# Twelve late result buffers, a written-out end of attention and two routings in turn, in a fused attention and mixture-of-experts kernel

## The chip, the cores and the metric

The kernel runs on one core of a Trainium2 chip. The metric is the device time of one execution in microseconds (us). A core has several engines, each of which works off its own program in order: TensorE (PE) multiplies matrices and transposes, VectorE (DVE) and ScalarE (ACT) do elementwise work and reductions, GpSimd (POOL) does some elementwise work and issues DMAs, SyncE (SP) issues DMAs. Engines wait for one another, and for DMAs, at semaphores. In the profile a name such as SPq or ACTq is the queue on which an engine issues its transfers.

## What is computed

The reference has two parts. Attention works in chunks of 32 queries, each with 16 keys of left context, 8 of right context and 8 memory keys (B=4 batches, H=8 heads, S=768 positions, D=64). Its output, seen as x with N=3072 rows of 512 columns, goes through a router that picks two of E=8 experts for each token, and each expert is a two-layer network with 1024 hidden units:

```python
scores = scale * np.matmul(q_c, k_full.transpose(0, 1, 3, 2))
a = softmax(scores)                      # in the reference: max, exp, divide
out[:, :, c_start:c_end] = np.matmul(a, v_full)
...
x = attn_out.transpose(0, 2, 1, 3).reshape(B * S, H * D)
noisy_logits = x @ w_gate + np.log1p(np.exp(x @ w_noise)) * noise
top2 = np.argpartition(-noisy_logits, 2, axis=1)[:, :2]
top2_w = softmax(take_along_axis(noisy_logits, top2, axis=1))
for e in range(E):
    for k in range(2):
        mask = top2[:, k] == e
        h = np.maximum(x[mask] @ w1[e], 0.0)
        out[mask] += top2_w[mask, k, None] * (h @ w2[e])
```

## The kernel before

The whole body runs under a manual schedule: the order in which the code issues instructions is the order on each engine, and the framework only adds the waits between engines and hands out buffers from pools. When a pool's tile has several buffers (bufs=6), the writer of the seventh tile waits for the last reader of the first.

*Attention* runs over 16 pairs of heads (four per batch), as a pipeline in the loop at L754. A turn i of the loop issues the transposes of the probabilities of pair i-1 (PT_pe, with the copy PT_copy on ACT), the maximum and the subtraction of pair i (max_dve), transposes of q and k of pair i+2 (turn_pe), the product with v of pair i-1 (PV_pe), the exponential of pair i (exp_act), the router's logits of pair i-3 (logits_pe), the normalising multiply of pair i-1 (mult_dve), the transposes of the finished rows of pair i-2 (xT_pe) and the scores of pair i+1 (scores_pe). It also loads v on POOL's queue, and the first experts' weights at turns 10, 12 and 14. The loop has a 17th turn (i=16) in which only the parts for earlier pairs run.

*Routing* follows whenever four pairs of a batch have their logits (route, L353). It is cut into small steps: s1 exponential and logarithm on ACT; s1b, s2 noisy logits and their comparison on DVE; s2b which experts come first and second; s2c, s2d the gates' exponentials; s3 on PE the rank of every token in its expert's queue, which needs the counts of the batches before (`seen`); s4 the gates into the row and the store of the batch's rows to a table in DRAM (x_rows, L421; on SP's queue for batches 0 to 2, on ACT's for batch 3); s4b, s5, s5b, s5c ranks into slots (s5c on POOL); s6 on PE the table of which token sits in which slot; s7 its copy; s8 the update of `seen`, with `gap`, which closes slots that later batches may not use. For batches 0 to 2 these steps wait in a list (`pending`), from which steps() (L567) takes one or two groups per turn.

*Experts.* Each expert has 832 slots: six tiles of 128 and a seventh of 64. decode (L536) makes indices from the table. gather (L594) fetches a tile's rows from x_rows by an indirect DMA that POOL issues; 14 buffers hold what was fetched. turn (L611) transposes a tile on PE and copies it out on ACT or DVE, up (L634) is the first layer with its relu (from three PSUM banks, alternately on ACT and DVE), down (L652) the second layer: per tile eight matmuls into one of two banks, an eviction with the gate into a result tile `ys` (L660, six buffers; ACT for odd tiles at L672, DVE for even ones at L674), and a scatter-add of that tile into `out`, an indirect DMA on POOL (L675). The generator every (L690) orders all this. Experts 0 and 1 start before routing is complete: tiles 0 and 1 from batches 0 and 1 (idx_s), tiles 2 and 3 after batch 2 (idx_a), tiles 4 to 6 after batch 3 (idx_f). Experts 2 to 7 follow with seven tiles each; gathers run ahead by two to three sets, first-layer weights are loaded in down, second-layer weights between the gathers. units(k) takes k steps of this generator, so that expert work can be put between steps of routing by hand.

*Around the end of attention* (L798 to L833) the order in code is: after the last turn the PSUM banks of attention are given to the experts; decode for batch 2, the middle gathers (L807), the zero fills of `out` (L809: three DMAs of 2 MB on SP's queue from a zero tile zt), w2 of expert 1 (L811), the last logits, the turns of expert 1's first tiles on DVE, then batch 3's routing in five groups with expert units in between (L818), the half tile's fix, decode for all, and the gathers of sets 2 and 3. Then a new pool ("full", L838) takes the memory that attention's pool leaves.

*Overflow.* Between the second layers of sets 6 and 7, L843 to L859 find tokens that did not fit: `gov` is read back from the gate columns of x_rows (L849, a DMA on SP's queue), multiplied by `miss` (L851) and stored back (L872). A loop at the end (L884) would work on such tokens; with these inputs it ends at once.

Of the kernel before, what the change touches and what calls it, by code (L numbers as in the profile page):

```python
# [24 lines left out]
def kernel(  # L25
# [44 lines left out]
    SKIP = 32  # L70
    NEG = -1e30
# [16 lines left out]
    def body():  # L88
# [243 lines left out]
        def xT_pe(n):  # L332
# [4 lines left out]
            xt = ap_.tile([128, BT, 128], BF16, name="xt")  # L337
# [15 lines left out]
        def route(b):  # L353
# [61 lines left out]
            def s4():  # L415
# [5 lines left out]
                (nc.sync if b < B - 1 else nc.scalar).dma_start(out=xd_part[b][b * S:(b + 1) * S].rearrange("(t p) r -> p t r", p=128), in_=xrows[b])  # L421
# [49 lines left out]
            def s8():  # L471
# [8 lines left out]
                if b >= B - 3:  # L480
# [8 lines left out]
            if b == B - 1:  # L489
                return (s1,), (s1b, s2), (s2b, s3, s2c, s4b, s5, s5c), (s2d,), (s4, s5b), (s6, s7)  # L490
            if b == B - 3:
                return (s1,), (s1b, s2), (s2b, s2c, s2d), (s3, s4, s4b, spare_a), (s5, s5c, spare_b), (s5b, spare_c), (s6, s7, s8, spare_d, begin_first)
# [141 lines left out]
        def up(s, c0=0, c1=None):  # L634
# [5 lines left out]
            k = -(-(c1 - c0) // 512)  # L640
            for f in range(FB):
# [10 lines left out]
        def down(s, between=()):  # L652
            e, tiles = sets[s]
            ht = hts[s]
            for n, j in enumerate(tiles):
# [4 lines left out]
                ys = mp.tile([128, Dm], F32, name="ys", bufs=6)  # L660
# [93 lines left out]
        for i in range(NPAIR + 1):  # L754
# [4 lines left out]
            if i < NPAIR:  # L759
                max_dve(i)  # L760
# [4 lines left out]
            if i < NPAIR:  # L765
                steps(1)
            if i >= 1:
                PV_pe(i - 1)
            if i < NPAIR:
                exp_act(i)  # L770
            if i >= 3:
                logits_pe(i - 3)
                if (i - 3) % HP == HP - 1:
                    begin, *rest = route((i - 3) // HP)
                    begin[0]()
                    assert not pending
                    pending.extend(rest)
# [4 lines left out]
            if i >= 2:  # L782
                xT_pe(i - 2)
# [12 lines left out]
            steps(1 if i < NPAIR - 2 else 2)  # L796
            if i >= NPAIR - 1:
                units(FB // 2)  # L798
        assert not pending
        pctx.close()  # L800
# [4 lines left out]
        turns["ring"] = bankT[:2]  # L805
        decode(tabs[(B - 2) % 2][:, :EARLY * NT], idx_a, None)
        for s in range(EARLY):  # L807
            gather(s, range(FIRST, SEALED), idx_a)
        for x in range(3):  # L809
            zero_fill(8 * x, 8)  # L810
        load_w2(1)  # L811
        logits_pe(NPAIR - 2)
        xT_pe(NPAIR - 1)
        cnt["by"] = "dve"
        for j in range(FIRST):
            turn(1, j)
        logits_pe(NPAIR - 1)
        begin, *rest = route(B - 1)  # L818
        begin[0]()
        units(3)  # L820
        cnt["by"] = "act"
        for g, more in zip(rest, (3, 4, 1, 4, 1)):
            for fn in g:
                fn()
# [136 lines left out]
```

## Time and profile before

| what | value |
|---|---|
| three runs, us | 346.88, 347.7, 351.45 (median 347.7) |
| profiled execution, us | 351.4, of which 349.3 are the span of the core's instructions |
| mean granted TensorE clock | 0.928 |
| busy, share of the span | PE 79%, DVE 46%, ACT 43%, POOL 66% |
| DMA | 60.30 MB, mean 173 GB/s |

All positions in time below are us from the start of the profiled execution's span. A row of the timeline gives start, duration, engine, line and operation, then output<-inputs by the program's names with the shape, and in brackets the time that the engine was idle before it with what ended that wait. A row of the waits gives engine, tile and line, what released it, and then the total, the count and the longest. A row of the DMA issues gives the KB of one transfer and the median time from issue to landing. PEclk on the page is the TensorE clock that the throttle granted, in tenths of full speed, for 40 equal slices of the span.

### The profile page before, as it was taken

The numbers are of one execution on the slowest core, as the hardware profiler recorded it, in microseconds if no ns is written. First come the engines' busy times: TensorE is split into PE (matmuls) and PEld (weight loads), VectorE is DVE, ScalarE is ACT, GpSimd is POOL, SyncE is SP. The second block draws the span as 40 slices with busy tenths as digits, with TensorE's granted clock in tenths as the row PEclk, the third lists the DMA queues.
The fourth block names the chain that finished last, engine by engine and source line by source line (L and its number), as shares of the span: only waits on it lengthen the run. The fifth ranks groups of instructions, "written<-read, shape, count | busy, mean of one in ns | idle before, by whom it ended". The sixth has DMA issues, their size and how long they took to land. (4 is left out here: it accounts for less than half of the span.)

```text
span 349.3 us, 7639 instructions
## 1 busy us (share of the span) xinstructions
PE 277.5 (79%) x3071; PEld 175.5 (50%) x3085; DVE 161.4 (46%) x363; ACT 149.1 (43%) x295; POOL 228.9 (66%) x219
## 2 busy tenths in 40 slices
PE   0787687686667758795999999399999999999940
PEld 0765566575455545353555555255555555545420
DVE  7467569789784664221434343033343433324310
ACT  1689978868444543212343433223332432223110
POOL 8997777548323512787878686887887825656380
PEclk9999969969676999998999999889999999999995
DMA  9999999999989997499989999999999997959293
GB/s 113 161 149 186 164 166 186 195 127 213 185 154 376 380 226 143 96 140 226 209 161 190 214 195 211 204 175 193 202 200 192 179 145 111 124 65 139 27 138 45
DMA packets 99110, 60.30 MB, mean 173 GB/s; under 512 B 63488, under 2 KB 83968, under 8 KB 99072
## 3 DMA queue, kind: packets, MB, share of 16 engines
q0 software_dynamic: 82208, 49.84, 105.2%
q1 hardware_dynamic: 15792, 9.05, 9.0%
q10 hardware_dynamic: 1072, 0.88, 0.8%
q8 instruction: 26, 0.43, 0.5%
q14 instruction: 12, 0.10, 0.1%
HBM read 65.07 MB, written 23.27 MB: 253 GB/s over the span
## 5 line engine op out<-in xcount | busy, mean ns | idle before, releaser
L647 PEld LDWEIGHTS <-w1t 128*128 128x128 bf16 x576 | 57.5, 101 | 52.9 <-issue 11.8
L675 POOL DMA_INDIRECT out_dram<-ys,idx_f x40 | 62.8, 1570 | 31.8 <-DVE ys L674 20.7
L603 POOL DMA_INDIRECT xl<-x_rows,idx_f x48 | 49.8, 1037 | 28.7 <-DVE hts L632 10.8
L663 PE MATMUL bankE<-w2t,htf 128*128 128x512 bf16 x278 | 65.7, 379 | 0.5
L647 PE MATMUL bankE<-xTf,w1t 128*128 128x416 bf16 x256 | 52.0, 346 | 5.4 <-DVE xTf L624 5.4
L674 DVE TENSOR_SCALAR ys<-bankE,gt 128x512 f32<-128x512 f32 (+1 forms) x32 | 21.9, 684 | 69.3 <-PE bankE L663 49.8
L672 ACT ACTIVATE ys<-bankE,gt 128x512 f32<-128x512 f32 x24 | 16.5, 687 | 71.4 <-PE bankE L663 52.5
L133 POOL DMA_DIRECT2D vp<-in_v_dram x34 | 33.3, 987 | 15.3 <-PE bankO L316 4.9
L663 PEld LDWEIGHTS <-htf 128*128 128x128 bf16 x288 | 27.3, 98 | 28.8 <-issue 0.3
L630 ACT ACTIVATE htf<-bankE 128x416 bf16<-128x416 f32 x32 | 16.5, 517 | 34.7 <-PE bankE L647 34.7
L632 DVE TENSOR_SCALAR htf<-bankE 128x416 bf16<-128x416 f32 x32 | 18.9, 591 | 26.9 <-PE bankE L647 26.9
L647 PE MATMUL bankT<-xTf,w1t 128*128 128x416 bf16 x128 | 28.4, 345 | 0.3 <-DVE htf L632 0.3
L263 ACT COPY kT<-bankT 64x768 bf16<-64x768 bf16 x32 | 25.3, 791 | 6.2 <-PE bankT L253 5.8
L620 PE MATMUL bankT<-identb,xl 128*128 128x128 bf16 (+1 forms) x224 | 20.3, 219 | 5.5 <-DMA xl<-x_rows,idx_f 2.3
L620 PEld LDWEIGHTS <-xl 128*128 128x128 bf16 (+1 forms) x224 | 15.3, 99 | 16.1 <-issue 4.4
L663 PE MATMUL bankE<-w2t,hts 128*128 128x512 bf16 x92 | 21.5, 379 | 0.2
L647 PE MATMUL bankT<-xTs,w1t 128*128 128x256 bf16 (+1 forms) x88 | 15.2, 314 | 5.8 <-ACT hts L630 4.2
L287 DVE TENSOR_REDUCE mx<-bankS 128x12 f32<-128x768 f32 x16 | 15.2, 953 | 9.3 <-PE bankS L282 9.3
L647 PE MATMUL bankE<-xTs,w1t 128*128 128x256 bf16 (+1 forms) x104 | 16.0, 297 | 2.6 <-DVE xTs L624 1.3
L313 PE MATMUL bankO<-memv,PT 128*128 128x132 bf16 x96 | 9.9, 251 | 9.8 <-ACT PT L306 9.6
L289 DVE TENSOR_TENSOR sd<-bankS,mx 128x768 f32<-128x768 f32 x16 | 15.3, 958 | 1.8 <-DVE mx L287 0.5
L455 POOL TENSOR_TENSOR col<-mm_all,tl 128x672 f16<-128x672 f16 x4 | 6.7, 1670 | 14.4 <-DVE tl L442 14.4
(182 smaller groups left out, 456.0 us busy)
## 6 DMA issues: line engine op xcount, KB each, us to landing
w1t<-in_moe_w_dram POOLq DMA_DIRECT2D x8, 1024.0 KB, 12.1
w2t<-in_moe_w_dram POOLq DMA_DIRECT2D x8, 1024.0 KB, 11.3
out_dram<-zt SPq DMA_DIRECT2D x3, 2048.0 KB, 10.3
vp<-in_v_dram POOLq DMA_DIRECT2D x30, 168.0 KB, 8.6
qg<-in_q_dram POOLq DMA_DIRECT2D x16, 192.0 KB, 7.7
kg<-in_k_dram POOLq DMA_DIRECT2D x16, 192.0 KB, 8.0
x_rows<-xrow SPq DMA_DIRECT2D x3, 792.0 KB, 8.3
x_rows<-xrow ACTq DMA_DIRECT2D x1, 792.0 KB
```

What stands on the lines that cost most here:

```text
L133: nc.gpsimd.dma_start(out=vp[p0 + j:p0 + j + nj, c:c + m, hh, :], in_=bass.AP(v.tensor, v.offset + (hd * S + c * chunk + j - left_ctx) * D ...
L263: nc.scalar.copy(kbufs[n % 2][hs, hh].rearrange("d (p j) -> d p j", j=SJ), p_t[hs])
L289: nc.vector.tensor_tensor(out=sd, in0=st[n]["ps"], in1=mx.rearrange("p x (u o) -> p x u o", o=1).to_broadcast([128, 2, BT, CTX]), op=Alu.s ...
L603: nc.gpsimd.indirect_dma_start(out=xl, out_offset=None, in_=xd, in_offset=bass.IndirectOffsetOnAxis(ap=idx[:, c:c + 1], axis=0), bounds_ch ...
L620: nc.tensor.transpose(out=p_t[:, kp, :w], in_=xl[:w, kp * 64:(kp + 1) * 64].bitcast(BF16), identity=identb[:w, :w])
L630: nc.scalar.activation(out=dst, in_=src, func=Act.Relu)
L632: nc.vector.tensor_scalar(out=dst, in0=src, scalar1=0.0, scalar2=None, op0=Alu.max)
L647: nc.tensor.matmul(out=h[:, :hi - lo], lhsT=W1[e][:, kp, f * 128:(f + 1) * 128], rhs=xTs[s][:, kp, lo:hi], start=(kp == 0), stop=(kp == KP ...
L663: nc.tensor.matmul(out=y, lhsT=ht[:, f, o:o + w], rhs=W2[e][:, f, :], start=(f == 0), stop=(f == FB - 1))
L672: nc.scalar.activation(out=ys[:, :wide], in_=y[:, :wide], func=Act.Copy, scale=gate)
L674: nc.vector.tensor_scalar(out=ys[:, :wide], in0=y[:, :wide], scalar1=gate, scalar2=None, op0=Alu.mult)
L675: ins = nc.gpsimd.indirect_dma_start(out=rows, out_offset=bass.IndirectOffsetOnAxis(ap=idx, axis=0), in_=ys[:, :wide], in_offset=None, bou ...
```

## The change

Twelve result buffers instead of six, in the pool "full". Batch 3's rows are stored on SP's queue instead of ACT's. The update of `seen` (s8) is separated from `gap` (s8b), and for batch 1 it comes one group earlier. In up(), two blocks of at most 256 columns share a PSUM bank and one relu instruction, so a unit of the narrow sets now covers two blocks. The attention loop ends after turn 15; what turn 16 did is written out behind it, ahead of expert work, and the steps of batch 2's and batch 3's routing are called by name, in turn with the remaining parts of attention and with units. The zero fills are issued in the code at turn 14 (NPAIR - 2), and their only wait is for zt. The turns of expert 1's first tiles are no longer forced to DVE ahead of batch 3's routing; those of expert 0 stand between the last parts of attention. `gov` is set to zero on DVE before it is read back. The loop for tokens that did not fit takes its accumulator from another pool.

```diff
@@ -68,6 +68,7 @@
...
     SKIP = 32
+    NYS = 12
     NEG = -1e30
@@ -334,7 +335,7 @@
...
                 nc.tensor.transpose(out=p_x[:, t, :], in_=xrows[b][:, t, hp * 64:(hp + 1) * 64].bitcast(BF16), identity=identb)
-            xt = ap_.tile([128, BT, 128], BF16, name="xt")
+            xt = ap_.tile([128, BT, 128], BF16, name="xt", bufs=3)
             nc.scalar.copy(xt, p_x)
@@ -418,7 +419,7 @@
...
                 nc.vector.tensor_tensor(out=xrows[b][:, :, XC:].bitcast(F32), in0=ge, in1=bc(gs, E), op=Alu.mult)
-                (nc.sync if b < B - 1 else nc.scalar).dma_start(out=xd_part[b][b * S:(b + 1) * S].rearrange("(t p) r -> p t r", p=128), in_=xrows[b])
+                nc.sync.dma_start(out=xd_part[b][b * S:(b + 1) * S].rearrange("(t p) r -> p t r", p=128), in_=xrows[b])
@@ -477,7 +478,9 @@
...
                     nc.vector.tensor_copy(seen, sm)
-                if b >= B - 3:
+
+            def s8b():
+                if B - 3 <= b < B - 1:
@@ -486,10 +489,10 @@
...
-            if b == B - 1:
-                return (s1,), (s1b, s2), (s2b, s3, s2c, s4b, s5, s5c), (s2d,), (s4, s5b), (s6, s7)
+            if b >= B - 2:
+                return dict(s1=s1, s1b=s1b, s2=s2, s2b=s2b, s2c=s2c, s2d=s2d, s3=s3, s4=s4, s4b=s4b, s5=s5, s5b=s5b, s5c=s5c, s6=s6, s7=s7, s8=s8, s8b=s8b)
             if b == B - 3:
-                return (s1,), (s1b, s2), (s2b, s2c, s2d), (s3, s4, s4b, spare_a), (s5, s5c, spare_b), (s5b, spare_c), (s6, s7, s8, spare_d, begin_first)
+                return (s1,), (s1b, s2), (s2b, s2c, s2d), (s3, s4, s4b, spare_a), (s5, s5c, spare_b), (s5b, spare_c, s8), (s6, s7, s8b, spare_d, begin_first)
             return (s1,), (s1b, s2), (s2b, s2c, s2d), (s3, s4, s4b), (s5, s5c), (s5b,), (s6, s7, s8)
@@ -638,6 +641,18 @@
...
             k = -(-(c1 - c0) // 512)
+            w = c1 - c0
+            if 2 * w <= 512:
+                for f in range(0, FB, 2):
+                    h = hring[cnt["h"] % 3] if hring else tr()
+                    cnt["h"] += 1
+                    for x in range(2):
+                        for kp in range(KP):
+                            nc.tensor.matmul(out=h[:, x * w:(x + 1) * w], lhsT=W1[e][:, kp, (f + x) * 128:(f + x + 1) * 128], rhs=xTs[s][:, kp, c0:c1],
+                                             start=(kp == 0), stop=(kp == KP - 1))
+                    relu(hts[s][:, f:f + 2, c0:c1], h[:, :2 * w].rearrange("p (x w) -> p x w", w=w))
+                    yield "up", s, f
+                return
             for f in range(FB):
@@ -657,7 +672,7 @@
...
                 gate = gts[s][:, j:j + 1]
-                ys = mp.tile([128, Dm], F32, name="ys", bufs=6)
+                ys = pools["full"].tile([128, Dm], F32, name="ys", bufs=NYS)
                 if w == CAP:
@@ -751,35 +766,38 @@
...
                 scores_pe(0)
-        for i in range(NPAIR + 1):
+        late = {}
+        for i in range(NPAIR):
             if i + NQ < NPAIR:
...
                 PT_pe(i - 1)
-            if i < NPAIR:
-                max_dve(i)
+            max_dve(i)
             if i >= 1:
...
                 turn_pe(i + 2, 0)
-            if i < NPAIR:
-                steps(1)
+            steps(1)
             if i >= 1:
                 PV_pe(i - 1)
-            if i < NPAIR:
-                exp_act(i)
-            if i >= 3:
+            exp_act(i)
+            if 3 <= i < NPAIR - 1:
                 logits_pe(i - 3)
                 if (i - 3) % HP == HP - 1:
-                    begin, *rest = route((i - 3) // HP)
-                    begin[0]()
-                    assert not pending
-                    pending.extend(rest)
+                    b = (i - 3) // HP
+                    if b == B - 2:
+                        late[b] = route(b)
+                        late[b]["s1"]()
+                    else:
+                        begin, *rest = route(b)
+                        begin[0]()
+                        assert not pending
+                        pending.extend(rest)
             if i + 2 < NPAIR:
...
                 mult_dve(i - 1)
-            if i >= 2:
+            if 2 <= i < NPAIR - 1:
                 xT_pe(i - 2)
@@ -793,36 +811,56 @@
...
                 load_w2(0)
-            steps(1 if i < NPAIR - 2 else 2)
-            if i >= NPAIR - 1:
-                units(FB // 2)
+                for x in range(3):
+                    zero_fill(8 * x, 8)
+            steps(1)
         assert not pending
+
+        def do(r, *names):
+            for nm in names:
+                r[nm]()
+
+        n = NPAIR - 1
+        r2 = late[B - 2]
+        PT_pe(n)
+        PT_copy(n)
+        xT_pe(n - 2)
+        do(r2, "s1b", "s2")
+        PV_pe(n)
+        mult_dve(n)
+        xT_pe(n - 1)
+        logits_pe(n - 3)
+        logits_pe(n - 2)
         pctx.close()
...
         turns["ring"] = bankT[:2]
+        do(r2, "s2b", "s2c")
+        turn(0, 0)
+        xT_pe(n)
+        logits_pe(n - 1)
+        do(r2, "s3", "s4b", "s8")
+        turn(0, 1)
+        do(r2, "s2d")
+        logits_pe(n)
+        r3 = route(B - 1)
+        do(r3, "s1")
+        do(r2, "s5", "s5c", "s8b", "s5b", "s4")
+        units(4)
+        do(r2, "s6", "s7")
         decode(tabs[(B - 2) % 2][:, :EARLY * NT], idx_a, None)
...
             gather(s, range(FIRST, SEALED), idx_a)
-        for x in range(3):
-            zero_fill(8 * x, 8)
         load_w2(1)
-        logits_pe(NPAIR - 2)
-        xT_pe(NPAIR - 1)
-        cnt["by"] = "dve"
-        for j in range(FIRST):
-            turn(1, j)
-        logits_pe(NPAIR - 1)
-        begin, *rest = route(B - 1)
-        begin[0]()
+        do(r3, "s1b", "s2", "s2b", "s2c")
+        units(4)
+        do(r3, "s3", "s4b", "s2d", "s5", "s5c", "s4")
         units(3)
-        cnt["by"] = "act"
-        for g, more in zip(rest, (3, 4, 1, 4, 1)):
-            for fn in g:
-                fn()
-            units(more)
+        do(r3, "s5b")
+        units(1)
+        do(r3, "s6", "s7")
         tab = tabs[(B - 1) % 2]
@@ -846,6 +884,7 @@
...
         gov = lp.tile([128, NP, E], F32, name="gov")
+        nc.vector.memset(gov, 0.0)
         nc.sync.dma_start(out=gov, in_=xd[:, XC:].rearrange("(t p) e -> p t e", p=128).bitcast(F32))
@@ -903,7 +942,7 @@
...
             bounds_check=N - 1, oob_is_err=True)
-        o = mp.tile([128, Dm], F32, name="ys", bufs=6)
+        o = lp.tile([128, Dm], F32, name="o")
         nc.gpsimd.indirect_dma_start(
...
             bounds_check=N - 1, oob_is_err=True)
```

## The prediction, made before the changed kernel was run

> **What bounds the kernel now.** I read the page's slices first, then the waits of TensorE (PE), then the timeline around each long wait, then GpSimd's (POOL's) timeline and the DMA issues. From 137.6 to the end PE is busy in nearly every slice, so what it waits for there is time. The waits of PE after 100 us: line, what ended the wait, total, times, longest.
>
> ```profile
> PE bankE L647 <- DVE xTf L624: 5.4, 1, 5.4
> PE bankT L647 <- ACT hts L630: 4.2, 1, 4.2
> PE bankT L620 <- DMA xl<-x_rows,idx_f: 2.3, 3, 1.3
> ```
>
> The two long ones are named after a relu and a copy, but the timeline shows what these were late for (start, duration, engine; in brackets the idle time before it and its releaser).
>
> ```profile
> 160.60 0.69 ACT L672 ACTIVATE ys<-bankE,gt 128x512 f32<-128x512 f32 x1 [7.52 <-DMA out_dram<-ys,idx_a]
> ...
> 161.67 0.79 PE L647 MATMUL bankT<-xTs,w1t 128*128 128x320 bf16 x4 [4.23 <-ACT hts L630]
> ```
>
> ```profile
> 225.67 0.48 DVE L674 TENSOR_SCALAR ys<-bankE,gt 128x256 f32<-128x256 f32 x1 [7.74 <-DMA out_dram<-ys,idx_f]
> ...
> 226.41 2.96 PE L647 MATMUL bankE<-xTf,w1t 128*128 128x416 bf16 x8 [5.40 <-DVE xTf L624]
> ...
> 229.16 1.49 PE L647 MATMUL bankT<-xTf,w1t 128*128 128x416 bf16 x4
> ```
>
> An eviction waits for a result buffer (ys, six of them) whose scatter has not landed; copies and relus queue behind it, and PE behind these. The scatters are late because POOL issues without a gap, one per 1.87 us, from the first final gather at 137.55 to 281:
>
> ```profile
> 224.31 1.57 POOL L675 DMA_INDIRECT out_dram<-ys,idx_f  x1 [0.30 <-issue]
> ...
> 226.19 1.56 POOL L675 DMA_INDIRECT out_dram<-ys,idx_f  x1 [0.30 <-issue]
> ```
>
> What starts that sequence is the end of routing. Batch 2's rows are stored at 103.81, zero fills follow on the same queue, the middle gathers go at 116.50, batch 3's rows at 129.32, and the final gathers when these have landed:
>
> ```profile
> 103.81 0.36 SPq L421 DMA_DIRECT2D x_rows<-xrow  x1
> ...
> 104.26 5.45 SPq L576 DMA_DIRECT2D out_dram<-zt  x3
> ...
> 116.50 1.12 POOL L603 DMA_INDIRECT xl<-x_rows,idx_a  x1 [7.23 <-DVE idx_a L546]
> ...
> 129.32 0.41 ACTq L421 DMA_DIRECT2D x_rows<-xrow  x1
> ...
> 137.55 1.13 POOL L603 DMA_INDIRECT xl<-x_rows,idx_f  x1 [10.78 <-DVE hts L632]
> ```
>
> A late stretch matters for the added memset. VectorE (DVE) does the overflow bookkeeping between two expert layers, and PE loses 0.30 us there; the read of gov had been issued at 136.96, long before:
>
> ```profile
> 278.00 0.36 DVE L851 TENSOR_TENSOR gov<-gov,miss 128x192 f32<-128x192 f32 x1
> ...
> 278.86 0.58 DVE L632 TENSOR_SCALAR htf<-bankT 128x416 bf16<-128x416 f32 x1
> ...
> 279.50 0.86 PE L647 MATMUL bankT<-xTf,w1t 128*128 128x416 bf16 x4 [0.30 <-DVE htf L632]
> ```
>
> DMA prices (KB each, median us to landing):
>
> ```profile
> w2t<-in_moe_w_dram POOLq DMA_DIRECT2D x8, 1024.0 KB, 11.3
> out_dram<-zt SPq DMA_DIRECT2D x3, 2048.0 KB, 10.3
> x_rows<-xrow SPq DMA_DIRECT2D x3, 792.0 KB, 8.3
> nz_all<-in_moe_noise_dram SPq DMA_DIRECT2D x1, 96.0 KB, 5.8
> x_rows<-gov SPq DMA_DIRECT2D x1, 96.0 KB, 6.1
> ```
>
> **The change part by part.** The sum is made against the profiled execution: 351.4 us, of which 349.3 are the span. The three runs shown have a median of 347.7, 3.7 less; I take that off at the end.
>
> *Twelve ys buffers.* Both waits go: the writer then needs the scatter twelve tiles back, which by POOL's order had been issued 27 us or more before in both places. Gone are 4.23 and 5.40. After each, PE also ran at half clock for a while: four groups of 320 columns took 161.67 to 165.45, 3.78, where later ones take 0.54 each (2.15), so 1.6 more; three groups of 416 took 226.41 to 230.49, 4.08 for 2.11, so 2.0 more. Together 13.2. What is late next are the gathers, for POOL's work is the same and only starts with the stage. The seventh gather of expert 2 went out at 163.88 and landed 6.6 later, 170.5; PE used it at about 176.9. Moved by the stage's 4.1 (below) it lands at 166.4, and PE, earlier by 4.1 and 5.8, asks at 167.0; the ones before it land at 169.4 to 170.2 and are asked for two tiles earlier. I charge 1.0. The next sets land 1.5 us or more ahead. The new pool lies in memory that attention used; its last user, batch 3's row store, lands at about 133, before the first ys: nothing. Net -12.2.
>
> *End of attention.* Until 98.2 (multiply of pair 13) little changes; the earlier `seen` may save up to 1.2, not counted. Then DVE skipped from pair 14 to 2.9 us of batch 2's routing before pair 15's reduction; now pair 15 goes first. Reduction and subtraction (0.95, 0.96) end at 100.1, exp (0.84) at 101.0, transposes and copy (0.5, 0.8) at 102.3, PV (1.0) at 103.3, multiply (0.23, 0.96) at 104.5; pair 14's multiply and four routing steps fill DVE's gaps. Batch 2 still needs, on DVE in order: 1.4 (over to gd), 0.25 (rk), 0.4 (seen), 1.4 (r_all to tl), 0.6 (gap), 1.75 (Rn), 0.8 (ge to xrow): 6.6. Its row store leaves at 111.1, 7.3 later than before. Then transfers follow one another: landing 6.5 (this store took 5.7; the slowest of its kind 9.3), the first middle gather at 117.9, the fourth 4.05 later, landing 3.2 (a gather in an empty queue took 2.8 to 3.2, the middle ones beside the zero fills up to 7.7), and only now batch 3's store, which must wait for those gathers because it writes the table they read: 125.2. Its own DVE work (1.2, 2.9, 2.0 and 0.8 after 111.1) ends at 118, so the store no longer waits for it. Landing 8.0 as before (129.32 to 137.3; expert 1's w2t load is beside it again), issue 0.3: final gathers at 133.5 instead of 137.55, -4.1. With the shortest landings (5.7, 2.8, 5.7) it is -7.6, with the longest (9.3, 6.3, 9.3) +3.1. PE's first use of them moves alike.
>
> *Zero fills.* Their only wait is for zt (22.3), so SP issues them right behind batch 1's store, at 79.5, not at pair 14. SP has nothing else until 111. They now lie beside the v load of the last pair (83.83, landed after 8.7, used at 102.3), w1t of expert 1 (86.51, 11.5), the first gathers (92.1 to 96.3, used at 104) and w2t (97.3). Beside them a w2t load took 13.0 instead of 11.3, gathers up to 4 more: covered, 0; at worst 2, when the first gathers land after 104. At 111 the queue is free again if they sustain half the 400 GB/s they had from 108 to 120. The Trainium skill (DMA: Bandwidth & Descriptors, section Queues, rings and completion order) says each engine serves its queues in turn, a packet each. By it a load beside the fills would take up to twice as long, w1t 23 instead of 11.5, and land at 109.5, still before its use at 112: the sum would be the same, only the margin smaller.
>
> *Memset of gov.* The read now waits for it, and the memset stands in DVE's order behind the sixth full down-projection, so the read starts there and the multiply waits for it on DVE. Behind it wait four small operations and every second relu of the next layer; PE stops after the three banks are full, where it already lost 0.30. The read has 24 rows of 32 bytes per partition; the nearest rows of that shape are 5.8 (nz_all) and 6.1 (the store of gov), and I take 6.1. The memset (about 0.2) and the add of 0.36 beside it cancel: +6.0, and PE's half clock after such a wait another 2.0, as above: +8.0. Bounds: 2.8 (quickest gather), which costs 2.7 and no slow clock, and 12.5 (slowest v load), 14.4. The skill's price for one DMA (same page, section Anatomy of one DMA) is 2.0 us and bytes over 436 GB/s, 2.2 for these 96 KB; the sum would then be 5.9 us less.
>
> *The rest.* Relus of two blocks in one instruction: 16 of 512 columns for 32 of 256 (0.38 each), on ScalarE while PE needs 0.87 for the pair: covered, 0. The store moved from ACT's queue to SP's frees 0.41 of ACT: 0. POOL's order is the same throughout.
>
> Sum: -13.2 + 1.0 - 4.1 + 8.0 = -8.3: 343.1 against the profiled execution, 339.4 against the median.
>
> **The rivals.** (A) The gov read is quick or hidden: 2.2 to 3 us instead of 6.1, about 5.5 less, 334. For it: no other traffic on SP's queue. Against: both rows of that shape. (B) The end of attention gains nothing: three transfers in a chain where DVE work stood before, each with a long landing, +3.1 instead of -4.1: 346.6. For it: a store of 9.3 and gathers of 7.7 exist; against: these had heavy neighbours. (C) POOL is the bound, and the buffers only change what PE waits for. From 137.55 to 281 POOL has no gap, so each gather comes when POOL gets to it. If the gathers of experts 2 and 3 landed late enough to give back all 13.2, what is left is -4.1 + 8.0: 351.6, slower. It decides from 8.3 us of such waits on; against it stand the landings above, which leave at most 1. (D) The memory of the new pool makes the first evictions wait for attention's last readers: then ys at 135 waits some us; priced with B.
>
> **How the numbers follow.** Forecast 0.50; A 0.18; B (with D) 0.20; C 0.12. The forecast alone spans 336 to 343. The range reaches from A's lower part to B's upper one, 332 to 347. Two per cent, about what a measurement here tells from no change, is 340.7 and 354.7. Faster: two thirds of the forecast and A, 0.52; slower: the worse half of C, 0.06; the same: 0.42.
>
> **What would show it.** No eviction waits for out_dram near 157 or 221, and PE runs through; final gathers near 133.5, batch 2's store near 111, batch 3's 14 us behind it; zero fills at 79.5; one DVE wait of 6 us in gov's multiply, with PE idle about as long behind it and half clock after. Wrong would be: gathers named as PE's releaser for over 2 us in the full layers, a gov wait under 3, or a start of the final gathers after 138.

## The result, and the profile after the change

The changed kernel takes 360.56 us (median of four runs, 357.64 to 362.15); the kernel before, with one more run beside it, 348.62 (346.88 to 351.45). The ratio is 1.0325, 95% interval 1.0217 to 1.0433: slower by 3%, where 339.4 us were forecast. The profiled execution took 359.07 us, its span 357.4; before these were 351.4 and 349.3, so 8.1 us are to be found in the traces.

The waits of TensorE from 80 us on (columns as before: line, what ended the wait, total, times, longest):

```profile
PE bankE L662 <- DVE htf L635: 12.4, 1, 12.4
PE bankO L317 <- DMA vp<-in_v_dram: 7.5, 2, 4.4
PE bankT L623 <- DMA xl<-x_rows,idx_s: 3.3, 1, 3.3
PE bankT L623 <- DMA xl<-x_rows,idx_f: 2.5, 3, 1.2
PE bankT L623 <- DMA xl<-x_rows,idx_a: 2.4, 2, 1.5
```

The two waits for result buffers (5.4 and 4.2) are gone, as they should be. Three others stand in their place: attention waits for v, expert 0 waits for its first gathers, and one wait of 12.4 lies late in the expert layers.

The first two come from one place. The timeline from 79 us on:

```profile
79.20 11.17 SPq L579 DMA_DIRECT2D out_dram<-zt  x3
...
83.48 2.68 POOL L134 DMA_DIRECT2D vp<-in_v_dram  x3
...
102.84 0.83 PE L317 MATMUL bankO<-vp,PT 128*32 128x128 bf16 x24 [4.43 <-DMA vp<-in_v_dram]
103.06 1.01 POOL L606 DMA_INDIRECT xl<-x_rows,idx_s  x1 [7.82 <-DMA vp<-in_v_dram]
...
109.25 0.83 PE L317 MATMUL bankO<-vp,PT 128*32 128x128 bf16 x24 [3.04 <-DMA vp<-in_v_dram]
```

The zero fills go out at 79.2, as forecast. The load of v for the last pair, issued 4 us later, is what the matmul at 109.25 waits for; the matmul at 102.84 waits for the load before it. GpSimd itself stands for 7.8 us before the fourth gather until a load of v has landed, and so that gather is late twice. The instructions in the trace show why: GpSimd's DMAs use eight semaphores in turn, and each is issued only when the DMA that used its semaphore last, the eighth before it, has landed. Here that is a v load issued at 76.91, which landed at 102.80. The DMA issues of the changed kernel (KB each, median us to landing):

```profile
out_dram<-zt SPq DMA_DIRECT2D x3, 2048.0 KB, 17.6
...
vp<-in_v_dram POOLq DMA_DIRECT2D x2, 161.0 KB, 14.9
...
xl<-x_rows,idx_s POOLq DMA_INDIRECT x4, 21.4
xl<-x_rows,idx_a POOLq DMA_INDIRECT x4, 2.8
```

and the same rows of the kernel before:

```profile
vp<-in_v_dram POOLq DMA_DIRECT2D x2, 161.0 KB, 6.8
...
xl<-x_rows,idx_s POOLq DMA_INDIRECT x4, 4.7
xl<-x_rows,idx_a POOLq DMA_INDIRECT x4, 6.7
```

The row of v is the median of one load at the start (5.7 us in both kernels) and one of the last pair, and that one took 24.1 instead of 8.0. What lies beside the fills takes about 2.4 to 5 times as long; the middle gathers, now without them, take 2.8 instead of 6.7. The end of routing follows from there:

```profile
122.34 11.98 SPq L422 DMA_DIRECT2D x_rows<-xrow  x2
```

```profile
126.92 1.11 POOL L606 DMA_INDIRECT xl<-x_rows,idx_a  x1 [7.32 <-DVE m L396]
...
145.26 1.13 POOL L606 DMA_INDIRECT xl<-x_rows,idx_f  x1 [10.97 <-DMA x_rows<-xrow]
...
153.28 1.63 POOL L690 DMA_INDIRECT out_dram<-ys,idx_a  x1 [0.30 <-issue]
```

Batch 2's rows leave at 122.3 (the first of the two stores; the second at 134.0), the final gathers start at 145.26 and the first scatter at 153.28. Before these were 103.8, 137.55 and 145.56: the stage is 7.7 us late. From the first scatter to the end of the span it is 204.1 us, before 203.7. So all of the loss is made by 145 us, and behind it the change gives and takes the same. What it takes is the read of gov. VectorE and TensorE there:

```profile
271.76 0.22 DVE L887 MEMSET gov<- 128x192 f32 x1
...
284.40 0.36 DVE L890 TENSOR_TENSOR gov<-gov,miss 128x192 f32<-128x192 f32 x1 [12.21 <-DMA gov<-x_rows]
```

```profile
272.63 0.87 PE L662 MATMUL bankE<-xTf,w1t 128*128 128x416 bf16 x4
285.90 1.54 PE L662 MATMUL bankE<-xTf,w1t 128*128 128x416 bf16 x4 [12.40 <-DVE htf L635]
287.24 1.59 PE L662 MATMUL bankT<-xTf,w1t 128*128 128x416 bf16 x4
288.62 2.82 PE L662 MATMUL bankE<-xTf,w1t 128*128 128x416 bf16 x8
291.28 0.87 PE L662 MATMUL bankT<-xTf,w1t 128*128 128x416 bf16 x4
```

The read is issued at 272.12 and the multiply waits 12.2 us for it. TensorE fills its three banks, stops for 12.4, and then needs 5.4 us for four groups that take 0.7 each at full clock, 2.6 more (its granted clock was 0.51 in these 5.4 us, 1.00 behind them): 15 us in all.

### The profile page after: what moved, and what is told of

Its sections match the earlier page's. It is cut to its first block, busy times and chain, and to the rows that moved or that the text cites. A ratio compares the mean times of both kernels' runs of the same rounds, so it can differ in the third digit from the quotient of the medians.

```text
span 357.4 us, 7604 instructions
## 1 busy us (share of the span) xinstructions
PE 280.0 (78%) x3071; PEld 178.3 (50%) x3085; DVE 160.3 (45%) x355; ACT 149.6 (42%) x288; POOL 227.6 (64%) x219
## 5 line engine op out<-in xcount | busy, mean ns | idle before, releaser
L662 PEld LDWEIGHTS <-w1t 128*128 128x128 bf16 x448 | 44.1, 99 | 46.5 <-issue 15.8
L662 PE MATMUL bankE<-xTf,w1t 128*128 128x416 bf16 x256 | 52.7, 348 | 12.4 <-DVE htf L635 12.4
L651 PEld LDWEIGHTS <-w1t 128*128 128x128 bf16 x128 | 14.4, 113 | 6.9 <-issue 2.3
L317 PE MATMUL bankO<-vp,PT 128*32 128x128 bf16 x384 | 10.4, 254 | 8.4 <-DMA vp<-in_v_dram 7.5
L635 DVE TENSOR_SCALAR htf<-bankT 128x416 bf16<-128x416 f32 x16 | 9.5, 592 | 15.1 <-PE bankT L662 15.1
## 6 DMA issues: line engine op xcount, KB each, us to landing
w1t<-in_moe_w_dram POOLq DMA_DIRECT2D x8, 1024.0 KB, 12.1
```

What stands on the lines that cost most here:

```text
L635: nc.vector.tensor_scalar(out=dst, in0=src, scalar1=0.0, scalar2=None, op0=Alu.max)
L662: nc.tensor.matmul(out=h[:, :hi - lo], lhsT=W1[e][:, kp, f * 128:(f + 1) * 128], rhs=xTs[s][:, kp, lo:hi], start=(kp == 0), stop=(kp == KP ...
```

## The experiments

Each set of runs went to one chip, beside runs of the kernel before on the same chip; chips differ by 1% or so, so results are given as ratios to before with 95% intervals. "First scatter" and "rest" are from each run's trace: the time of the first scatter into `out`, and from there to the end of the span. Together they say in which of the two stages a difference lies.

| kernel | ratio to before | first scatter | rest |
|---|---|---|---|
| before, first trace; second trace | 1 | 145.6; 143.3 | 203.7; 201.1 |
| changed, first trace | 1.0325 (1.0217 to 1.0433) | 153.3 | 204.1 |
| changed, again | 1.0289 (1.0215 to 1.0362) | 155.1 | 204.9 |
| before + 12 buffers | 0.9814 (0.9704 to 0.9924) | 148.4 | 197.4 |
| before + 18 buffers | 0.9801 (0.9733 to 0.9868) | 144.3 | 196.0 |
| before + early fills | 1.0115 (1.0022 to 1.0208) | 154.5 | 203.7 |
| before + memset of gov | 1.0275 (1.0200 to 1.0349) | 146.4 | 208.1 |
| order and paired relus alone | 1.0193 (1.0091 to 1.0295) | 149.0 | 202.9 |
| changed, fills put back | 1.0124 (1.0016 to 1.0233) | 153.0 | 205.4 |
| changed, no memset | 1.0022 (0.9977 to 1.0067) | 155.3 | 197.3 |
| changed, no fills at all | 0.9964 (0.9895 to 1.0034) | 140.8 | 206.1 |
| changed, six buffers | 1.0548 (1.0427 to 1.0670) | 154.6 | 211.7 |

**The two kernels again**, for traces beside the parts.

> The kernel before, unchanged, for a trace on the same chip as the others of this set. All theories: 350 to 355 as the runs of before on that chip, two waits of PE for result buffers of 4 to 6 us, final gathers at 137 to 142.

> The changed kernel, unchanged, beside the parts. If the parts add up (result buffers -5.2, early fills +5.1, memset of gov +10 as the difference of the changed kernel and the one without it, the order about 1), it is 10 to 12 us above before on this chip, 362 to 365. If they do not, the difference is a matter of the chip.

One look at before gave 346.53 us, with waits for buffers of 6.6 and 1.6, final gathers at 135.3. The changed kernel came out at 360.79. The parts below, taken one at a time from the kernel before, add up to -1.9 + 1.2 + 2.8 + 1.9 = +4.0%, the whole is +2.9% to +3.3%: as good as their intervals allow.

**Result buffers alone**, on the kernel before, twelve and eighteen.

```diff
-                ys = mp.tile([128, Dm], F32, name="ys", bufs=6)
+                ys = pools["full"].tile([128, Dm], F32, name="ys", bufs=12)
```

> The kernel before with one part of the change alone: twelve ys buffers in the pool that opens after attention. Theory: both waits of PE (4.2 and 5.4) and the half clock behind them (3.6) go, 1 comes back as a wait for gathers: 12 us less than before, about 336. Rival: GpSimd is the bound, and PE waits as long for gathers of experts 2 and 3: 0 to 4 us less, 344 to 348.

> The kernel before with eighteen ys buffers (twelve gave 5.2 us where 12 were forecast). If evictions still waited for buffers with twelve, eighteen give 2 us or more beyond that, 7 to 12 us less than before. If GpSimd's pace or something else at the set starts gave the rest back, the result is that of twelve: 4 to 6 us less than before.

Both give 2%, 6.5 to 7 us, and eighteen give no more than twelve. Neither theory had it right: it is not 12, and not 0 to 4. With eighteen TensorE does gain what was forecast for twelve: its last matmul ends at 322.1, that is 177.9 us after the first scatter, before at 336.0, 190.4 after it: 12.5 sooner, for 12.2 forecast. But the rest of the span shrinks by only 7.7. With twelve the last matmul ends 185.6 us after the first scatter, only 4.8 sooner; three of the experts' first layers take 13.2 to 13.8 us there, for 11.4 to 12.0 with eighteen, and what holds them is open (in the changed kernel, with twelve too, the first two of them take 11.4). The rest of the span is 197.4 all the same. GpSimd's last three sets in the kernel with eighteen buffers:

```profile
284.81 1.59 POOL L675 DMA_INDIRECT out_dram<-ys,idx_f  x1 [3.41 <-DVE ys L674]
...
295.96 1.55 POOL L675 DMA_INDIRECT out_dram<-ys,idx_h  x1 [0.30 <-issue]
301.64 1.55 POOL L675 DMA_INDIRECT out_dram<-ys,idx_f  x1 [4.13 <-DVE htf L632]
...
312.79 1.55 POOL L675 DMA_INDIRECT out_dram<-ys,idx_h  x1 [0.30 <-issue]
320.69 1.55 POOL L675 DMA_INDIRECT out_dram<-ys,idx_f  x1 [6.35 <-DVE ys L674]
...
331.84 1.55 POOL L675 DMA_INDIRECT out_dram<-ys,idx_h  x1 [0.30 <-issue]
```

The last scatter goes out 9.7 us behind the last matmul. The releasers named had long been done: the first scatter of a set waits until the scatters of the set before have landed (the code ties them, because both add to the same rows), and the gaps are the landing of the last one. That is a chain of its own. A run that shortens it, by leaving out the seven scatters of the last set but one (their rows stay unadded):

```diff
+                if s == NS - 2:
...
+                    yield "down", s, j
+                    continue
                 ins = nc.gpsimd.indirect_dma_start(
```

> The kernel before with eighteen ys buffers and without the seven scatters of the last set but one (their rows stay unadded; gathers, layers and evictions are as they were; the last set's first scatter then waits for the scatters of the set ahead of that). Theory: once the buffers are there, GpSimd's chain of gathers and scatters sets the end, 204 to 205.5 us from the first final gather to the end in three kernels, and in its last part each set's first scatter waits for the landing of the whole set before. Without one set of it the end comes with TensorE: 5 to 8 us less than with eighteen buffers alone, 12 to 15 less than before. Rival: TensorE sets the end also with the buffers; then the time is that of eighteen buffers alone, 6 to 8 less than before.

336.53 us, 0.9619 (0.9478 to 0.9759) of before; its rest is 189.0 instead of 196.0. TensorE's last matmul stays where it was, 177.1 us after the first scatter, so it is not a faster TensorE: GpSimd's chain it is. With enough buffers and no wait for gov the rest is 195 to 199 us in all nine kernels that have both, whatever the first stage does. An attempt to shorten the gaps in earnest, with the half tile first in each set so that a whole tile is the last to land:

```diff
-            for n, j in enumerate(tiles):
+            for n, j in enumerate(tiles[-1:] + tiles[:-1] if tiles[-1] == NT - 1 else tiles):
```

> The kernel before with eighteen ys buffers, and in each set the half tile goes first in the second layer and in the scatters. Theory: GpSimd's chain sets the end, and in its last three sets it stands still for 3.4, 4.1 and 6.4 us until the last scatter of the set before, the half tile's, has landed (7.4 to 7.8 us; a whole tile's takes 5.8 to 6.2). With the half tile first a whole tile's scatter is the last: 1.5 to 2 us less in each of two or three sets, 3 to 6 us less than with eighteen buffers alone, 10 to 13 less than before. Rival: TensorE or another engine sets the end there, then no change, 6 to 8 less than before.

0.9856 (0.9762 to 0.9950), rest 199.1: nothing won. The gaps are 4.1, 5.4 and 7.7 us; the last scatter of a set lands no sooner than before. What makes it late is open: it is not that the tile is a half one.

**Early zero fills alone**, and taken out of the changed kernel in two ways.

```diff
             if i == NPAIR - 2:
                 load_w2(0)
+                for x in range(3):
+                    zero_fill(8 * x, 8)
...
             gather(s, range(FIRST, SEALED), idx_a)
-        for x in range(3):
-            zero_fill(8 * x, 8)
```

> The kernel before with one part of the change alone: the zero fills issued in the code at pair 14. Theory: they do here what they do in the changed kernel, the last v load takes over 20 us and the first gathers too, and the final gathers move from 137.6 to 142 to 147: 4 to 9 us more than before, 352 to 357. Rival: the harm needs the new order, in which everything waits for pair 15; in the old order expert work stands beside it: within 2 us of before.

1.0115; the final gathers start at 146.5, and TensorE waits 8.1 us for expert 0's first gathers. The harm does not need the new order. In the changed kernel, put back (and batch 3's store back on ACT's queue):

```diff
                 load_w2(0)
-                for x in range(3):
-                    zero_fill(8 * x, 8)
...
             gather(s, range(FIRST, SEALED), idx_a)
+        for x in range(3):
+            zero_fill(8 * x, 8)
```

> The changed kernel with the zero fills back behind the middle gathers' code and batch 3's store back on ACT's queue, the rest as changed. Theory: the early fills made the last v load (24.4 us to landing for 8.7) and the first gathers (21 to 23 for 3 to 6) late, and that alone moved the stage; the v wait of PE (7.5) is gone, the middle gathers start at 114 to 118 and the final gathers at 134 to 139 instead of 145.3: 6 to 11 us less than the changed kernel, 348 to 353. Rival: the written-out order is what is slow (batch 2's store at 122 because DVE and PE work through pair 15 first); then the final gathers stay within 2 us of 145 and so does the time.

1.0124, final gathers at 144.95: attention runs through, but the stage is as late as with early fills, by other waits. Batch 2's rows leave at 112.9; TensorE then waits 7.2 us for the middle gathers, and batch 3's rows, stored at 129.8 beside expert 1's w2t load, land 15 us later. So this run does not tell the theories apart. The next does: the fills left out.

```diff
                 load_w2(0)
-                for x in range(3):
-                    zero_fill(8 * x, 8)
```

> The changed kernel without the zero fills (the output then holds what the memory held, plus the sums). It prices the step that the prediction set at nothing. Theory: the last v loads land in 7 to 9 us, the first gathers in 3 to 6, batch 2's rows leave at 110 to 112 and the final gathers start at 130 to 134 instead of 145 to 147: 12 to 15 us less than the changed kernel, 346 to 350 where before is 350 (the wait for gov stays). Rival: the written-out order is what is late; then the final gathers start after 140 and 5 us or less are won.

The final gathers start at 132.78, 12.5 us earlier than in the changed kernel's first trace (the forecast of the order had 133.5), and the time is 3.2% less than that of the changed kernel (0.9964 against 1.0289). The line that answers to the one at 145.26 above:

```profile
132.78 1.12 POOL L606 DMA_INDIRECT xl<-x_rows,idx_f  x1 [10.90 <-DVE hts L635]
```

**The order alone**: the edit with the fills put back, and two more.

```diff
-    NYS = 12
+    NYS = 6
...
-        nc.vector.memset(gov, 0.0)
```

> The changed kernel with three parts undone: six ys buffers, no memset of gov, zero fills behind the middle gathers' code and batch 3's store on ACT's queue. What is left is the order at the end of attention and the paired relus. If the order gains 4 us as forecast, 345 to 348 where before is 350. If its chain of transfers gives the gain back (batch 3's rows took 15 us to land in the kernel with the fills put back, beside the zero fills and expert 1's w2t load), the final gathers start at 143 to 146 and the time is 3 to 8 us above before.

1.0193, final gathers at 140.97. The order needs a quiet queue behind batch 2's store, and the fills lie just there: the middle gathers take 7.5 us, batch 3's store 14. Without any fill the final gathers start 2.5 to 4.8 us earlier than in the two traces of before, with the fills there 3.4 to 5.7 later.

**The memset alone**, on the kernel before, and taken out of the changed kernel.

```diff
+        nc.vector.memset(gov, 0.0)
         nc.sync.dma_start(out=gov, in_=xd[:, XC:]...)
```

> The kernel before with one part of the change alone: the memset of gov ahead of its read. Theory: the read starts where the memset stands in VectorE's order, behind the sixth full down-projection, and takes 12 us beside the gathers' and scatters' traffic; PE stands for about that and runs at half clock behind it: 10 to 15 us more than before. Rival: in the kernel before GpSimd sets the pace there, so most of it is hidden: under 5 us more.

> The changed kernel without the memset of gov, so that its read is issued when batch 3's rows have landed. Theory: the wait of 12.4 us of PE near 274 is gone with about 2.6 of half clock behind it: 15 us less than the changed kernel, about 344. Rival: GpSimd's chain of gathers and scatters sets the end, and the wait only hid that; then PE waits for gathers of the last two experts instead and 5 us or less are won.

On before 1.0275, 9.6 us (7.0 to 12.3). The wait on VectorE is 6.1 us, as forecast, TensorE's 6.3, and the layer takes 19.5 us instead of 11.8, 7.7 more; so about the 8.0 of the forecast is what the memset does there. In the changed kernel it costs 2.7% (1.0022 against 1.0289), 7 to 8 us of the rest (197.3 against 204.1 and 204.9): that lies between the 15 of the theory and the 5 of its rival. Of the 15 us that TensorE loses, about half would have been lost to GpSimd's chain anyway. The wait is twice as long there. What GpSimd has under way at the read, in the changed kernel (read at 272.12) and in before with the memset (read at 276.99):

```profile
269.28 0.98 POOL L564 DMA_DIRECT2D w2t<-in_moe_w_dram  x1
...
274.69 1.01 POOL L606 DMA_INDIRECT xl<-x_rows,idx_f  x1 [0.30 <-issue]
276.00 1.63 POOL L690 DMA_INDIRECT out_dram<-ys,idx_f  x1 [0.30 <-issue]
```

```profile
276.36 1.73 POOL L675 DMA_INDIRECT out_dram<-ys,idx_f  x1 [0.30 <-issue]
278.40 1.55 POOL L675 DMA_INDIRECT out_dram<-ys,idx_h  x1 [0.30 <-issue]
279.39 1.55 POOL L561 DMA_DIRECT2D w2t<-in_moe_w_dram  x1
```

With twelve buffers TensorE runs ahead of GpSimd and reaches the read when a weight load has just been issued and gathers are still to come; in before with the memset only scatters are under way, and the weight load follows 2.4 us behind the read. A run with six buffers in the changed kernel:

```diff
-    NYS = 12
+    NYS = 6
```

> The changed kernel with six ys buffers instead of twelve. If the buffers are worth here what they are in the kernel before (6 to 7 us), it is that much slower. Theory: less, because with six buffers TensorE reaches the read of gov when GpSimd's weight load and gathers are behind it, and the read takes 6 to 8 us instead of 12 to 13: 0 to 4 us slower than the changed kernel, 360 to 366 where before is 350.

```profile
DVE gov L890 <- DMA gov<-x_rows: 8.3, 1, 8.3
```

The wait falls from 12 or 13 to 8.3, as this explanation has it; here too the weight load comes only 3.2 us behind the read. The packets of the traces say the same. From the read's issue to its last packet it took 11.7 us in the changed kernel, while GpSimd's queue moved 2.23 MB; 8.0 with six buffers (1.01 MB); 5.8 in before with the memset (0.70 MB). Without the memset the same read goes out just ahead of the final gathers, and in the twelve traces where no fill lies before it on its queue it took 2.9 to 4.0 us (3.0 in the kernel before), with 0.07 to 0.22 MB beside it. No run changes the traffic alone. The time is 1.0548 of before, 8 to 9 us above the changed kernel, not 0 to 4: waits for buffers of 3.6 and 5.3 and their half clock are back in full. Together with the 4 us that the shorter read saves, the buffers are worth 12 to 13 us here. Where TensorE is held up by gov, GpSimd's chain is not the end, and the buffers are worth what the forecast said.

**Another place for the fills**, without the memset: behind batch 3's store; there, with expert 1's w2t load behind the first final gathers; at the start of attention in both orders, with eighteen buffers; and the w2t load ahead of the middle gathers in the old order, with eighteen buffers and the half tile first. The edits for the first two:

```diff
         do(r3, "s3", "s4b", "s2d", "s5", "s5c", "s4")
+        for x in range(3):
+            zero_fill(8 * x, 8)
```

```diff
-        load_w2(1)
...
             todo.extend((s, j) for j in sets[s][1])
+        load_w2(1)
```

> The changed kernel without the memset of gov and with the zero fills behind batch 3's store on SP's queue. Theory: no transfer of attention and no middle gather lies beside the fills; batch 2's rows leave at 111 to 113, batch 3's at 124 to 126, and only expert 1's w2t load is beside these: final gathers at 135 to 138, and 205 from there, 341 to 344 where before is 350. If the order itself is slow, they start after 142 and the time is 347 or more.

> As the one with the fills behind batch 3's store, and expert 1's w2t load moved behind the first six final gathers. Theory: batch 3's rows then land with nothing beside them, in 4 to 6 us instead of 11, final gathers at 129 to 132, 335 to 338 where before is 350, faster than both kernels. If the store's landing does not depend on that load, the time is that of the kernel with the fills alone moved.

1.0053 (1.0012 to 1.0094) and 1.0104 (1.0008 to 1.0199). The final gathers start at 133.48, sooner than the 135 to 138 expected, and at 130.66, as expected (before: 137.55 and 135.27); but then GpSimd's first scatter stands, in the first of the two:

```profile
151.90 1.62 POOL L690 DMA_INDIRECT out_dram<-ys,idx_a  x1 [10.71 <-DMA gov<-x_rows]
```

It adds to what the fills write and must wait for them (the read named lies directly behind them on the queue). The rest is 196.8 and 195.2.

The edit at the start of attention:

```diff
         nc.gpsimd.memset(zt, 0.0)
+        for x in range(3):
+            zero_fill(8 * x, 8)
```

> The changed kernel without the memset of gov, with eighteen ys buffers, and with the zero fills issued as soon as their zero tile is there (about 22 us), ahead of the attention loop. Without any fill the final gathers started at 132.8. Theory: at 22 us the loads of attention run several pairs ahead, so that part of the fills' 16 us of transfers is covered; attention ends 0 to 8 us later, the final gathers start at 133 to 141, and GpSimd's chain takes 204 to 207 from there: 337 to 348 where before is 350. Rival: attention is bound by its loads from the start; then all of the fills' time is added there, final gathers at 145 or later, 350 or more.

> The kernel before with eighteen ys buffers and the zero fills at about 22 us, in the old order. Theory: the middle gathers land in 3 us instead of 7.6 and expert 1's w2t load in 10 to 11 instead of 14, batch 3's rows land 2 to 4 us sooner; against it stands what attention loses at 22 to 40 us (0 to 8): 338 to 348 where before is 350. Rival: attention loses the fills' whole 16 us, 350 or more.

1.0221 (1.0175 to 1.0267) and 1.0098 (1.0050 to 1.0146): the rival was right. TensorE waits 12.1 and 11.5 us for one v load, from 41 and 43 us on; in the first of the two:

```profile
PE bankO L317 <- DMA vp<-in_v_dram: 12.1, 1, 12.1
```

And the w2t load moved:

```diff
         assert not pending
+        load_w2(1)
         pctx.close()
...
-        load_w2(1)
         logits_pe(NPAIR - 2)
```

> As the kernel with eighteen buffers and the half tile first, and expert 1's w2t load moved ahead of the middle gathers, where GpSimd stands idle. Theory: batch 3's rows then land with little beside them, 5 to 6 us instead of 8.6, the final gathers start 2 to 4 us earlier and with them the whole chain: 13 to 16 us less than before. If the load beside the zero fills delays the middle gathers as much, nothing more than with the half tile first.

0.9942 (0.9900 to 0.9983), final gathers at 138.63: beside the fills the load took 19.7 us, the middle gathers 13 to 15 and TensorE waited 7.1 for them. Batch 3's rows did land quickly, in 4.1 us, but they left 5.1 us later (at 134.0; 128.9 with the half tile first alone). The fastest kernel of the study that computes the whole result is before with eighteen buffers, 342.98 us beside 351.13.

## Why the prediction was wrong, step by step

**Zero fills: "covered, 0; at worst 2".** This is the step that failed most. They took 12 to 14 us from the stage (the final gathers start at 145.3 and 147.1 in two traces of the changed kernel, at 132.8 without fills). The working gave attention's last v load its landing of 8.7 us and a use at 102.3, and asked only how much slower loads had been beside fills: w2t 13.0 for 11.3, gathers up to 4 more. Those rows were of transfers that met only the second half of the fills or their end (the fills' packets ran from 107.2 to 126.2 us there). Beside all of them the v load took 24.4, w1t of expert 1 28.0 for 11.5, the first gathers 21 to 23. The Trainium skill's rule (DMA: Bandwidth & Descriptors, section Queues, rings and completion order) that each engine serves its queues in turn, a packet each, agrees with the trace. Packets, MB and share of 16 engines of SP's queue (q1) and GpSimd's (q0) from 90 to 100 us, while the fills ran:

```profile
q1 hardware_dynamic: 1575, 3.17, 91.8%
q0 software_dynamic: 1576, 0.17, 27.4%
```

There were as many packets of the one as of the other. But "up to twice as long" follows only for packets of one length; here a packet of the fills is 2 KB and one of the v loads 128 bytes. In 6.5 us beside the fills (85.5 to 92) GpSimd's queue moved 1060 packets, in 6.5 us of the kernel before (83.5 to 90) 4594. The factor of two was applied to w1t alone, with 23 us as the result, where the trace has 28.0; for the v load it would have given 17.4 and a landing at 101.2, still ahead of its use. So the factor itself was wrong, for the load with the least slack most of all. Nor was it asked what else GpSimd holds back: its next issue stood for 7.8 us until a slow load had landed.

**End of attention: -4.1.** The order of the chain was right. Without fills the final gathers start at 132.78, 133.5 were forecast; that they agree so closely is partly luck, as errors of its terms cancel. Its terms: batch 2's store to the first middle gather 4.6 us (6.8 forecast), from there to batch 3's store 7.0 (7.3), and that store to the final gathers 11.3 (8.3), 22.9 together in the changed kernel for 22.4. The start was wrong, 122.3 for 111.1, which is the fills. "With the longest +3.1" was not wide enough, since it took no fills into account.

**Memset of gov: +8.0, bounds 2.7 and 14.4.** The mechanism is as described, on VectorE, TensorE and the clock. The term was mis-sized: TensorE lost 15.0. The read took 12.2 instead of 6.1, at the upper bound, and in every trace in which it took 12.1 to 13.2 it lay beside a weight load and gathers; with the memset alone, in the kernel before, it took 6.1. The 6.1 of the working came from rows of the same shape, and neither it nor rival A asked what GpSimd would have under way at the read. Rival A's 2.2 to 3 us is about what the read takes with almost nothing beside it: 3.0 us to its last packet where the kernel before issues it. The 2.2 us that the prediction names beside it are, in that section of the Trainium skill (DMA: Bandwidth & Descriptors, section Anatomy of one DMA), the price of a DMA that GpSimd issues; this read goes out on SP's queue, and no run shows it below 2.9.

**Twelve buffers: -13.2, and 1.0 given back by gathers.** In the changed kernel the waits went as said, and gathers cost 2.5 us against 2.3. What was not seen is that GpSimd's chain alone needs 195 to 199 us from the first scatter to the end, only 2 to 9 less than the whole kernel before took (201.1 and 203.7), so that what TensorE gains beyond that does not show in the time. Rival C had the right engine at the wrong place: it looked for late gathers, and it was the scatters, each set waiting for the landing of the one before. Alone the buffers are worth 6.5 to 7 us. In the changed kernel gov hid this. (GpSimd's pace in the working, one issue per 1.87 us without a gap, is that of scatters; gathers follow at about 1.3, and there are three gaps of 1.0 to 1.7 us. The sum does not hang on it.)

**Relus, store queue, turns: 0.** Nothing in the traces speaks against it; they were not tried by themselves.

The sum by the changed kernel's own trace: -13.2 for the buffers, +7.7 for the stage, +15.0 for gov, 0.2 for gathers, +9.7 against +8.1 measured; 1.6 us are not assigned. Against the forecast of -8.3 the stage is off by 11.8 and gov by 7.0.

## What to carry to other kernels

A bulk transfer without a deadline is not free because its queue is empty: price it by what lies beside it on the DMA engines, and for each of these transfers ask when its result is used, starting with the one with the least slack. Where two queues get as many packets each, the one with the smaller packets gets the fewer bytes: compare the packets' sizes first. When a wait is removed, ask how long the next chain takes by itself; here the scatters, with 195 to 199 us, kept about half of the gain. A wait that is added costs what its transfer takes at that moment, among the traffic that the other edits of the same change put there.

## What the runs showed of the hardware beyond that

Behind three fills of 2 MB the transfers that GpSimd issued next landed 16 to 17 us late, whatever their size: two v loads (24.4 us for 8.7, 24.1 for 8.0), the weight load of 1 MB behind them (28.0 for 11.5) and the first three gathers behind that (21.0 to 23.0 for 4.2 to 6.3). The gathers landed 0.3 to 1.1 us after the weight load in both kernels, so they were late with their queue and not by themselves. The fills' packets ran from 85.5 to 106.9 us, those of the v loads until 108.8. The read of gov, 96 KB in 32-byte pieces, took 2.9 to 4.0 us to its last packet with almost nothing beside it; VectorE waited 6.1 and 8.3 us for it where only scatters were under way at its issue and a weight load followed, and 12.1 to 13.2 in four traces where a weight load had been issued 2.2 to 3.8 us before it, with gathers behind. A slow load also blocked GpSimd, which issued no further DMA for 7.8 and 4.1 us: both times the DMA that had to land was the eighth before, as the program's semaphores have it. Batch 3's row store took from 4.1 us (with expert 1's w2t load moved ahead, from 134.0 to 138.1, when that load and the gathers had landed) to 15 us (with the fills put back), by what shared the engines with it.
